# V of the last block's two groups issued from GpSimd's queue instead of SyncE's

## The chip, the cores and the metric

The kernel runs on one core of a Trainium2 chip. A core has a tensor engine (TensorE, PE in the profile; its weight loads are listed as PEld), a vector engine (VectorE, DVE), a scalar engine (ScalarE, ACT), GpSimd (POOL) and SyncE (SP), which does nothing but issue DMA transfers. Each engine works through its own list of instructions in order; engines wait for each other by semaphores. Transfers are moved by 16 DMA engines of the core, whichever engine issued them. The metric is the device time of one execution in microseconds (us), the median of several.

## The reference

Attention within chunks of 64 positions, over 8 batches, 8 heads, 576 positions and a head size of 64, and then a feed-forward part with a squared ReLU on the 4608 x 512 result:

```python
q_c, k_c, v_c = (z.reshape(B, H, S // 64, 64, D) for z in (q, k, v))
scores = np.matmul(q_c, k_c.transpose(0, 1, 2, 4, 3)) / np.sqrt(D)
attn = np.exp(scores - scores.max(-1, keepdims=True))
attn = attn / (attn.sum(-1, keepdims=True) + 1e-09)
x = np.matmul(attn, v_c)            # (B, H, S, D) -> (B*S, H*D) = (4608, 512)
h = np.maximum(x @ w_in, 0.0)       # w_in: 512 x 2048
out = (h * h) @ w_out               # w_out: 2048 x 512
```

All inputs and the output are float32 in HBM.

## The kernel before

The 4608 tokens are cut into 18 groups of 256 (`GT`), each of four chunks of 64; two groups make a block, so there are nine blocks, 0 to 8. Groups are numbered from 0 as well: block 8 holds groups 16 and 17, block 7 groups 14 and 15. Most groups are four neighbouring chunks of one batch ("whole"); groups 14 and 15 are gathered from the ninth chunk of each batch, so their loads come in twice as many pieces.

For one group the steps are: load Q, K and V; cast Q and K to bfloat16 (`CQ`, `CK`; both: `C`; lines L449 and L454, on GpSimd for the blocks that matter here); transpose both by one DMA (`TD`, L460, issued by SyncE); scores on TensorE and the exponential on ScalarE (`SC`, L483 and L494); the product with V in two halves (`AV0`, `AV1`, L510), with a division by the sums on VectorE (L442, L443); and the transpose of the result x (`XT`), which for blocks 6 to 8 is a DMA that SyncE issues (L535). The attention of block j+1 is done while the feed-forward part of block j runs.

V of a group lies in SBUF in float32. The even heads go to `v_even[g % 5]` in two pieces of 128 tokens (L308); the odd heads go to tiles of `v_odd`, shifted by a chunk (L312). Group 16 has three odd pieces (64, 128 and 128 tokens), group 17 two (128 and 64). One piece of 128 tokens and four heads is 128 KB, in runs of 256 bytes. Each DMA waits until the readers of the buffer's earlier contents are through.

From block 4 on the feed-forward part works in "quads": a quad is a quarter of the hidden units of a block, and its products are Strassen-like, seven instead of eight (`quad_step`, L657), with sums of x formed by VectorE in `x_sums` (L614). The second of these sums, e2, needs both groups' transposed x of its block, and the product A6 uses it. A quad is spread over one tick of four slots; a block has four quads and so 16 slots. `run(tick)` emits, slot by slot, the quad's products, the second layer's products of the block before (L780), and whatever `plan` has for the slot. At the start of each tick GpSimd squares one ReLU result of the quad before (L676). Stores of results are issued by GpSimd (L809, or L804 for the gathered groups).

The order on each engine's list is thus written out by hand: `at(j, s, f)` puts f at slot s of block j, and a slot above 15 is one of block j+1. The loads of block j+2 are put into the slots of block j. For j = 6 (`n_blk - 3`), which loads block 8, the pieces come from one iterator, `pieces`: Q and K of group 16 (three DMAs), Q and K of group 17 (three), V of group 16 (five), V of group 17 (four); `load(n, more)` issues the next n of them. All are on SyncE, among the transposes that stand in the same slots: XT of group 14 at slot 8 and of group 15 at slot 13, TD of group 16 at 9.5 and of group 17 at 14.5. AV0 of group 16 is planned at slot 2 of block 7, that of group 17 at slot 8.

Of the kernel before, what the change touches and what calls it, by code (L numbers as in the profile page):

```python
# [144 lines left out]
def kernel(  # L145
# [9 lines left out]
    nc = tc.nc  # L155
# [12 lines left out]
    blocks = [[g, g + 1] for g in range(0, n_grp, 2)]  # L168
# [8 lines left out]
    def is_whole(g):  # L177
        return chunks[g][0][0] == chunks[g][3][0]

    FIRST_DMA_T = 4
    X_BY_DMA = (6, 7, 8)
    QUADS = 4
    LEAD = 4
# [61 lines left out]
    def runs(g):  # L247

        for t in range(2):
            (b, s), (b1, s1) = chunks[g][2 * t:2 * t + 2]  # L250
            if b == b1:
                yield t, 0, 2 * CH, b, s
            else:
                yield t, 0, CH, b, s
                yield t, CH, CH, b1, s1
# [6 lines left out]
    def qk_pieces(g):  # L262


        def pairs(which, src, p, m, b, s):
            return lambda: nc.sync.dma_start(  # L266
                out=loaded(g, which)[p:p + m // 2, :].rearrange("p (h e) -> p h e", h=H),
                in_=src[b, :, s:s + m, :].rearrange("h (s i) d -> s h (i d)", i=2))
# [3 lines left out]
        else:  # L272
            for c in range(4):
                yield pairs(0, q, c * CH // 2, CH, *chunks[g][c])
        if g < FIRST_DMA_T:
            yield pairs(1, k, 0, GT, *chunks[g][0])
# [9 lines left out]
    for g in range(n_grp):  # L286
        if is_whole(g):
# [3 lines left out]
            b, s = chunks[g][0]  # L291
# [12 lines left out]
    def v_pieces(g):  # L304

        even, odd = [], []
        for t, p, m, b, s in runs(g):
            even.append(lambda t=t, p=p, m=m, b=b, s=s: nc.sync.dma_start(  # L308
                out=v_even[g % NV][p:p + m, t, :, 0:D],
                in_=v[b, 0::2, s:s + m, :].rearrange("h s d -> s h d")))  # L310
        for n, p, m, b, s in odd_loads[g]:
            odd.append(lambda n=n, p=p, m=m, b=b, s=s: nc.sync.dma_start(  # L312
                out=v_odd[n % NO][p:p + m, :, 0:D],
                in_=v[b, 1::2, s:s + m, :].rearrange("h s d -> s h d")))
        if g < 2:
            yield from [even[0], *odd[:-1], even[1], odd[-1]]
        else:
            yield from even + odd
# [34 lines left out]
    def x_tile(j):  # L353
        if j not in xTs:
            xTs[j] = att_pool.tile([128, BT // 128, n_dt, 128], BF16, name="xT", bufs=2)
        return xTs[j]
# [107 lines left out]
    def scores(g):  # L464
        qkT = state.pop(("qkT", g))
        by_plane = g >= FIRST_DMA_T

# [62 lines left out]
    def transpose_x(g):  # L530
        x = state.pop(("x", g))
        n = 2 * half_of(g)
        dst = x_tile(g // 2)[:, n:n + 2].rearrange("p t h q -> p (t h) q")
        if g // 2 in X_BY_DMA:
            nc.sync.dma_start_transpose(out=dst, in_=x.rearrange("p t h a d -> p (t h a d)"))  # L535
# [15 lines left out]
    for j in range(n_blk):  # L551
        if j < QUADS:
            at = {(th, fh, h): 4 * th + 2 * fh + h
                  for th in range(2) for fh in range(2) for h in range(2)}
        else:
# [6 lines left out]
            at = {(*key, 0): s for key, s in zip(keys, old)}  # L562
# [83 lines left out]
    def tock():  # L646
        state["clock"] += 1
        for x in [x for x in later if x[0] <= state["clock"]]:
            later.remove(x)
            x[1]()  # L650
# [276 lines left out]
    def pieces(grps):  # L927
        for g in grps:
            yield from qk_pieces(g)
        for g in grps:  # L930
            yield from v_pieces(g)
# [72 lines left out]
    for j in range(QUADS):  # L1004
# [3 lines left out]
        def at(slot, f, *x):  # L1008
            plan.setdefault(slot, []).append((f, x))
# [28 lines left out]
        else:  # L1038
# [4 lines left out]
            if j == 2:  # L1043
                loads, go_slots = itertools.chain(*map(v_pieces, nxt), pieces(far)), [
                    *range(16), *range(27, 36)]
                slots = {SC: (6, 10), AV: (12, 22), XT: (15, 28), CQ: (20, 22), CK: (21, 24), TD: (24, 26)}
                for f in (CQ, CK, TD):
                    for i, g in enumerate(far):
                        at(slots[f][i], f, g)
                phases.append(out_j)  # L1050
            else:
                loads, go_slots = pieces(far), range(11)
                at(11, C, far[0])
                at(13, CQ, far[1])
                at(13, TD, far[0])
                slots = {SC: (2, 2), AV: (6, 10), XT: (13, 15)}
# [40 lines left out]
    for j in range(QUADS, n_blk):  # L1097
        if j == QUADS:
            n = 14 - LEAD
            slots = [1 + 19 * i // n for i in range(n)]  # L1100
            assert len(slots) == n
        else:
            slots = [s for s in range(4, 20) if s % 16 not in NO_OUT]
            start = 3
        if j == QUADS:
            g = blocks[QUADS + 1][1]
            between = {0: [(CK, (g, nc.scalar.copy)), (TD, (g,))]}
            for n in (0, 1, 2, 3):
                between.setdefault(n, []).append((load, (1, loads)))
            for n in (2, 2, 2, 3):  # L1110
                between.setdefault(n, []).append((x_sums, (QUADS, len([1 for z in between.values() for y in z if y[0] is x_sums]))))
            for f, x in between.get(0, []):
                f(*x)
            for i in range(LEAD):
                next(out_j)
                tock()
                for f, x in between.get(i + 1, []):
                    f(*x)
        else:
            outs[j - 1] = ffn_out(j - 1)  # L1120
            at(j, start, lambda j=j: next(outs[j - 1])())
        for s in slots:
            plan.setdefault(("out", 16 * (j - QUADS) + s), []).append(outs[j - 1])

        if j + 1 < n_blk:
            S0, V0, V1, X0 = ((1.5, 3.5), (4.5, 7.5), (6, 10), (8.5, 12)) if j == QUADS else (
                (1.5, 7), (3.5, 8), (5, 9.5), (5.5, 10)) if j == QUADS + 1 else (
                (0.5, 7), (2, 8), (3.5, 9.5), (3.5, 10)) if is_whole(blocks[j + 1][0]) else (
                (3.5, 9.5), (5, 11), (7, 12), (8, 13))
            for i, g in enumerate(blocks[j + 1]):  # L1130
                at(j, S0[i], SC, g)
                at(j, V0[i], AV0, g)
                at(j, V1[i], AV1, g)
                at(j, X0[i], XT, g)
            if j + 2 == n_blk:
                at(j, 22, check_sums)
                at(j, 25.5, count_bad)
            for i, s in enumerate((13.5, 16 if j == n_blk - 3 else 15, 17.5, 18)):
                at(j, s, x_sums, j + 1, i)
        if j == QUADS:  # L1140
            for s in range(4):
                at(j, 4 * s + 2, w_sums_in_place, s)
            assert next(loads, None) is None
        if j + 2 < n_blk:
            more = pieces(blocks[j + 2])
            if j == n_blk - 3:

                for s, n in ((0, 1), (1, 1), (2, 1), (8.5, 3), (13, 5), (15, 2), (15.5, 2)):
                    at(j, s, load, n, more)
            else:  # L1150
                for s in range(0, 16):
                    at(j, s, load, 1 if is_whole(blocks[j + 2][0]) else 2, more)
            for i in range(2):
                at(j, (9, 10 if j == QUADS else 13)[i], C, blocks[j + 2][i])
                at(j, ((9.5, 14.5) if j == n_blk - 3 else (12, 13.5))[i], TD, blocks[j + 2][i])
# [66 lines left out]
```

## Time and profile before

| | us |
|---|---|
| median of 3 runs | 277.8 |
| lowest and highest | 277.05, 279.23 |
| the profiled execution, its own time | 276.91 |
| its span in the trace | 275.1 |
| granted TensorE clock in it | 1.00 |

In the profile, a line such as L460 is the line of the kernel's text; SPq marks an issue by SyncE, whose time is that of the issue and not of the transfer. A DMA issued by GpSimd counts as busy time of POOL. Rows of the timeline give start and duration in us, engine, line, operation, what is written and read, and how many rows were merged; in square brackets stand the engine's idle time before it and what ended it. Rows of stretches give the busy time of PE, PEld, DVE, ACT and POOL with the number of instructions, then the granted clock, the share of time in which the 16 DMA engines were busy (packets that overlap count twice, so it can exceed 1), and the GB/s moved. The chain of waits follows the program back from its end, at each step to what released it.

Where the bytes go, by queue (packets, MB, share of 16 engines' time):

```profile
q1 hardware_dynamic: 133248, 46.54, 74.0%
q0 software_dynamic: 2624, 8.39, 9.6%
```

The first is SyncE's queue, the second GpSimd's, which carries stores alone.

### The profile page before, as it was taken

How to read it: one execution, taken by the hardware profiler on the slowest of the kernel's cores; microseconds unless marked ns; L12 is line 12 of the kernel's file. 1: busy time of each engine (PE TensorE's matmuls, PEld its weight loads, DVE VectorE, ACT ScalarE, POOL GpSimd, SP SyncE). 2: the span in 40 equal slices, each digit the busy share in tenths (PEclk: the TensorE clock that was granted, in tenths of full speed). 3: DMA queues.
4: the chain of work that ended last, by engine and by line, in shares of the span. 5: the costliest groups of instructions: out<-in, count | busy, mean ns of one | idle time of the engine just before them, and what ended most of it. 6: DMA issues, size and time to landing. Idle time of an engine off the chain costs nothing.

```text
span 275.1 us, 7923 instructions
## 1 busy us (share of the span) xinstructions
PE 264.9 (96%) x3261; PEld 203.4 (74%) x3261; DVE 199.2 (72%) x365; ACT 168.3 (61%) x300; POOL 89.6 (33%) x122
## 2 busy tenths in 40 slices
PE   2999999999999999999999999999999999999995
PEld 2764445888774588447878888888888888888884
DVE  1457514999538592499989998799779877994752
ACT  1657614894458883877678765565746665756430
POOL 2048834240360012040245224551643212331600
PEclk9999999999999999999999999999999999999999
DMA  7999999999999999999999999697999530220223
GB/s 216 262 352 389 361 332 270 339 213 172 262 210 218 238 234 218 275 223 178 228 236 197 218 238 194 103 220 196 244 187 224 123 76 2 99 55 7 71 83 114
DMA packets 136056, 55.60 MB, mean 202 GB/s; under 512 B 104273, under 2 KB 131921, under 8 KB 136017
## 3 DMA queue, kind: packets, MB, share of 16 engines
q1 hardware_dynamic: 133248, 46.54, 74.0%
q0 software_dynamic: 2624, 8.39, 9.6%
q8 instruction: 26, 0.43, 0.6%
q10 hardware_dynamic: 144, 0.13, 0.1%
q14 instruction: 14, 0.11, 0.1%
HBM read 36.70 MB, written 9.44 MB: 168 GB/s over the span
## 4 chain that ended last, share of the span: by engine, by line
PE 87%; DMA 4%; SPq 3%; DVE 3%; ACT 1%; issue 1%; ACTq 0%; DVEq 0%
PE ps_ffn L657 22%; PE ps_out L780 22%; PE ps_ffn L579 17%; PE ps_ffn L780 14%; PE ps_ffn L901 5%; PE ps_att L510 3%; PE ps_att L540 2%; DMA vo_sb<-in_v_dram 2%; PE ps_att L483 2%; DMA xT<-x 2%; DVE gT L598 2%; SPq L266 1%; SPq L308 1%; SPq L312 1%; DVE x L443 1%; ACT e L494 1%
## 5 line engine op out<-in xcount | busy, mean ns | idle before, releaser
L579 PE MATMUL ps_ffn<-xT,w_in_bf 128*128 128x512 bf16 (+1 forms) x328 | 57.8, 333 | 0.0
L780 PEld LDWEIGHTS <-w_st 128*128 128x128 bf16 x512 | 48.9, 98 | 6.6 <-DVE w_st L614 0.5
L665 DVE CUSTOM_DVE_ANT_0 relu<-ps_ffn,w_st 128x512 f32<-128x512 f32 x60 | 39.3, 684 | 13.0 <-PE ps_ffn L657 11.6
L579 PEld LDWEIGHTS <-w_in_bf 128*128 128x128 bf16 x328 | 31.2, 98 | 21.6 <-POOL w_in_bf L334 0.2
L598 DVE TENSOR_TENSOR gT<-relu 128x256 bf16<-128x256 bf16 (+2 forms) x68 | 34.1, 537 | 17.8 <-ACT relu L590 17.3
L590 ACT ACTIVATE relu<-ps_ffn 128x256 bf16<-128x256 f32 (+2 forms) x82 | 39.4, 501 | 9.4 <-PE ps_ffn L579 8.6
L657 PE MATMUL ps_ffn<-qk_st,w_in_bf 128*128 128x256 bf16 x240 | 35.3, 273 | 0.1
L657 PEld LDWEIGHTS <-w_in_bf 128*128 128x128 bf16 x320 | 30.7, 98 | 4.1 <-issue 0.3
L809 POOL DMA_DIRECT2D out_dram<-o_sb x24 | 17.6, 733 | 43.6 <-DVE o_sb L614 23.3
L780 PEld LDWEIGHTS <-gT 128*128 128x128 bf16 x296 | 28.6, 98 | 3.3
L780 PE MATMUL ps_out<-w_out_bf,w_st 128*128 128x256 bf16 x240 | 30.8, 273 | 0.0
L699 ACT ACTIVATE w_st<-ps_ffn 128x512 f32<-128x512 f32 x20 | 11.9, 597 | 29.6 <-PE ps_ffn L657 29.6
L443 DVE TENSOR_TENSOR x<-ps_att,recs 128x512 bf16<-128x512 f32 x36 | 24.9, 692 | 1.2
L657 PEld LDWEIGHTS <-qk_st 128*128 128x128 bf16 x240 | 22.6, 98 | 3.2 <-DVE qk_st L614 0.3
L657 PE MATMUL ps_ffn<-xT,qk_st 128*128 128x256 bf16 x160 | 23.9, 273 | 0.0
L676 POOL TENSOR_TENSOR qk_st<-relu 128x512 bf16<-128x512 f32 x10 | 10.3, 1034 | 41.6 <-DVE relu L665 38.1
L494 ACT ACTIVATE e<-ps_att 128x1024 bf16<-128x1024 f32 x18 | 18.3, 1025 | 8.5 <-PE ps_att L483 8.5
L676 POOL TENSOR_TENSOR gT<-relu 128x512 bf16<-128x512 f32 x10 | 10.3, 1033 | 35.4 <-DVE relu L665 30.5
L449 POOL CAST qkb<-qk_st 128x1024 bf16<-128x1024 f32 x12 | 13.0, 1082 | 14.9 <-DMA qk_st<-in_q_dram 14.9
L674 ACT ACTIVATE gT<-relu 128x512 bf16<-128x512 f32 x28 | 17.7, 631 | 0.0
L780 PE MATMUL ps_ffn<-w_out_bf,w_st 128*128 128x256 bf16 x144 | 17.7, 273 | 0.0
L614 DVE TENSOR_TENSOR w_st<-gT,w_st 128x1024 bf16<-128x1024 bf16 x26 | 16.8, 682 | 0.0
(92 smaller groups left out, 428.7 us busy)
## 6 DMA issues: line engine op xcount, KB each, us to landing
qk_st<-in_q_dram SPq DMA_DIRECT2D x16, 512.0 KB, 5.6
out_dram<-o_sb POOLq DMA_DIRECT2D x28, 256.0 KB, 3.9
qk_st<-in_k_dram SPq DMA_DIRECT2D x24, 256.0 KB, 5.6
ve_sb<-in_v_dram SPq DMA_DIRECT2D x32, 128.0 KB, 3.9
w_st<-in_moe_w_in_dram SPq DMA_DIRECT2D x8, 512.0 KB, 5.9
w_st<-in_moe_w_out_dram SPq DMA_DIRECT2D x8, 512.0 KB, 5.5
vo_sb<-in_v_dram SPq DMA_DIRECT2D x24, 128.0 KB, 3.6
qk_st<-in_k_dram SPq DMA_DIRECT2D x4, 512.0 KB, 5.8
```

What stands on the lines that cost most here:

```text
L443: nc.vector.tensor_tensor(out=x, in0=o[:, :, :, 0:D], in1=rec.to_broadcast([128, 2, n, D]), op=ALU.mult)
L494: nc.scalar.activation(out=e_out, in_=s_in, func=AF.Exp, scale=scale)
L579: nc.tensor.matmul(out=h[:, 0:n], lhsT=w_in_bf[:, dt, ft * 128:(ft + 1) * 128], rhs=xT[:, c // 128:(c + n) // 128, dt, :], start=(dt == 0) ...
L590: nc.scalar.activation(out=rl[:, 0:n], in_=h[:, 0:n], func=AF.Relu)
L598: nc.vector.tensor_tensor(out=dst, in0=src, in1=src, op=ALU.mult)
L614: nc.vector.tensor_tensor(out=out, in0=in0, in1=in1, op=op)
L657: nc.tensor.matmul(out=bank[:, f * GT:(f + 1) * GT], lhsT=a[:, dt, ft * 128:(ft + 1) * 128], rhs=b[:, :, dt, :], start=(first and f == 0 a ...
L665: nc.vector._custom_dve(TENSOR_ADD_SAT, out=out, in0=in0, in1=in1, s0=BIG, s1=0.0)
L674: engine.activation(out=dst, in_=r, func=AF.Square)
L676: engine.tensor_tensor(out=dst, in0=r, in1=r, op=ALU.mult)
L780: nc.tensor.matmul(out=out_ps, lhsT=lhsT, rhs=b[:, i, :], start=(first and i == 0 and (last or t == 0)), stop=(i == HF - 1), skip_group_ch ...
L809: dma.dma_start(out=out[t0:t0 + GT, col:col + HD].rearrange("(t p) d -> p t d", p=128), in_=o_sb.rearrange("p (t d) -> p t d", d=HD))
```

## The change

V of groups 16 and 17 is issued by GpSimd. The five pieces of group 16 stand at slot 4.5 of block 6 instead of slot 13, where they were behind XT of group 15; the four of group 17 stand at slot 18 of block 6, which is slot 2 of block 7, instead of slots 15 and 15.5. Q and K of both groups keep their slots and their order on SyncE.

```diff
@@ -180,6 +180,7 @@
     FIRST_DMA_T = 4
+    V_BY_GPSIMD = (16, 17)
     X_BY_DMA = (6, 7, 8)
@@ -304,12 +305,13 @@
     def v_pieces(g):
 
         even, odd = [], []
+        dma = nc.gpsimd if g in V_BY_GPSIMD else nc.sync
         for t, p, m, b, s in runs(g):
-            even.append(lambda t=t, p=p, m=m, b=b, s=s: nc.sync.dma_start(
+            even.append(lambda t=t, p=p, m=m, b=b, s=s: dma.dma_start(
                 out=v_even[g % NV][p:p + m, t, :, 0:D],
                 in_=v[b, 0::2, s:s + m, :].rearrange("h s d -> s h d")))
         for n, p, m, b, s in odd_loads[g]:
-            odd.append(lambda n=n, p=p, m=m, b=b, s=s: nc.sync.dma_start(
+            odd.append(lambda n=n, p=p, m=m, b=b, s=s: dma.dma_start(
                 out=v_odd[n % NO][p:p + m, :, 0:D],
                 in_=v[b, 1::2, s:s + m, :].rearrange("h s d -> s h d")))
@@ -1144,9 +1146,11 @@
         if j + 2 < n_blk:
             more = pieces(blocks[j + 2])
             if j == n_blk - 3:
-
-                for s, n in ((0, 1), (1, 1), (2, 1), (8.5, 3), (13, 5), (15, 2), (15.5, 2)):
-                    at(j, s, load, n, more)
+                more = itertools.chain(*map(qk_pieces, blocks[j + 2]))
+                last_v = itertools.chain(*map(v_pieces, blocks[j + 2]))
+                for s, n, which in ((0, 1, more), (1, 1, more), (2, 1, more), (4.5, 5, last_v),
+                                    (8.5, 3, more), (18, 4, last_v)):
+                    at(j, s, load, n, which)
```

## The prediction, made before the changed kernel ran

> **What bounds the kernel now.** I read the page first, then the waits of TensorE in the middle of the program, then the chain of waits around the one wait that was left, and last the two issuing queues around it.
>
> ```profile
> span 275.1 us, 7923 instructions
> PE 264.9 (96%) x3261; PEld 203.4 (74%) x3261; DVE 199.2 (72%) x365; ACT 168.3 (61%) x300; POOL 89.6 (33%) x122
> ```
>
> TensorE is busy for 264.9 of 275.1 us, so 10.2 us of idle time is all that any change of order could give back, and it matters where those 10.2 us lie. The waits of PE alone, asked for 130 to 258 us (the quad stage, in which blocks 4 to 8 run and all that the diff moves is issued), answer with one row:
>
> ```profile
> PE ps_ffn L657 <- DVE qk_st L614: 0.2, 1, 0.2
> ```
>
> In 128 us TensorE waited once, for 0.2 us. The other idle time lies in the first loads and the last block, which the diff does not touch. The chain of waits around that one wait shows what it hangs on (start, duration, what):
>
> ```profile
> 201.12 4.81 DMA xT<-x
> ...
> 206.02 0.56 DVE qk_st L614
> ...
> 206.62 1.05 PE ps_ffn L657 x8
> ```
>
> The transposing DMA of x of block 7's second group (I call it XT15) is issued at 201.12, lands 4.81 us later at 205.93, VectorE forms the sum e2 from it until 206.58, and the A6 product of block 7's first quad starts at 206.62. There is no slack: a microsecond more on XT15's landing is a microsecond of idle TensorE, while a microsecond less gives 0.2 us. SyncE's queue shows what stands ahead of XT15 and what behind:
>
> ```profile
> 188.18 0.61 SPq L266 DMA_DIRECT2D qk_st<-in_q_dram  x1
> 188.85 2.31 SPq L279 DMA_DIRECT2D qk_st<-in_k_dram  x2
> 191.32 2.76 SPq L535 DMA_TRANSPOSE xT<-x  x1
> 194.13 0.58 SPq L266 DMA_DIRECT2D qk_st<-in_q_dram  x1
> 194.75 1.49 SPq L279 DMA_DIRECT2D qk_st<-in_k_dram  x2
> 196.50 4.52 SPq L460 DMA_TRANSPOSE qkT<-qkb  x1
> 201.12 1.74 SPq L535 DMA_TRANSPOSE xT<-x  x1
> 202.91 1.37 SPq L308 DMA_DIRECT2D ve_sb<-in_v_dram  x2
> 204.33 1.83 SPq L312 DMA_DIRECT2D vo_sb<-in_v_dram  x3
> 206.26 3.53 SPq L460 DMA_TRANSPOSE qkT<-qkb  x1
> 209.84 2.09 SPq L308 DMA_DIRECT2D ve_sb<-in_v_dram  x2
> 211.97 1.86 SPq L312 DMA_DIRECT2D vo_sb<-in_v_dram  x2
> 213.93 1.37 SPq L535 DMA_TRANSPOSE xT<-x  x1
> ```
>
> In order: Q and K of group 16, XT14, Q and K of group 17, the transpose of group 16's Q and K (TD16), XT15, then V of group 16, TD17, V of group 17, XT16. From 188.18 to 206.16 the list never stands still for more than 0.3 us. The nine V loads that leave it all stand behind XT15.
>
> **The change, part by part.** First, what SyncE loses: five issues between 202.91 and 206.16 and four between 209.84 and 213.83. XT15 is ahead of them, so its issue gains nothing. TD17 can rise by at most 206.26 − 202.91 = 3.35 us, and nothing in the waits shows TensorE standing for it; XT16 waits for its x in any case. Gain on the path: nothing.
>
> Second, what GpSimd gains. Its own list around the two places, with its idle time in brackets:
>
> ```profile
> 184.04 1.03 POOL L676 TENSOR_TENSOR qk_st<-relu 128x512 bf16<-128x512 f32 x1 [3.21 <-DVE relu L665]
> 185.02 0.75 POOL L809 DMA_DIRECT2D out_dram<-o_sb  x1
> 190.95 1.03 POOL L676 TENSOR_TENSOR qk_st<-relu 128x512 bf16<-128x512 f32 x1 [5.18 <-DVE relu L665]
> 192.74 1.54 POOL L449 CAST qkb<-qk_st 128x1024 bf16<-128x1024 f32 x1 [0.77 <-DMA qk_st<-in_q_dram]
> 195.43 1.04 POOL L454 CAST qkb<-qk_st 128x1024 bf16<-128x1024 f32 x1 [1.15 <-DMA qk_st<-in_k_dram]
> ...
> 205.25 1.04 POOL L676 TENSOR_TENSOR gT<-relu 128x512 bf16<-128x512 f32 x1 [2.92 <-DVE relu L665]
> 206.23 1.47 POOL L809 DMA_DIRECT2D out_dram<-o_sb  x2
> 212.02 1.03 POOL L676 TENSOR_TENSOR gT<-relu 128x512 bf16<-128x512 f32 x1 [4.32 <-DVE relu L665]
> ```
>
> Squares fall at the start of each tick of four slots. The casts of group 16 are planned at block 6's slot 9 and stand behind the square at 190.95, which is therefore that of slot 8; the one at 184.04 is that of slot 4, and the one at 205.25, two ticks after 190.95, that of slot 16. The five loads of group 16 therefore come after 184.04 + 1.03, with the store at 185.02 at their side, in the 5.18 us that GpSimd then stood idle; the four of group 17 come beside the two stores at 206.23, in the 4.32 us before 212.02.
>
> No load by GpSimd is in the trace. Its nearest rows are its stores; L804 writes 128 rows of 1 KB and L809 256 of them (duration in ns, lowest, median, highest):
>
> ```profile
> L809 POOL DMA_DIRECT2D out_dram<-o_sb x24: 707/738/751, 69.9 to 239.0; - x24
> L804 POOL DMA_DIRECT2D out_dram<-o_sb x8: 603/612/656, 245.0 to 260.9; - x8
> ```
>
> 128 more rows cost 738 − 612 = 126 ns. A V load of 128 tokens is 4 heads x 128 = 512 rows of 256 bytes: 738 + 2 x 126 = 990 ns is my estimate; one of 64 tokens has 256 rows, 738 ns. Bounds for the large one: 612 ns if rows did not count, 2 x 738 = 1476 ns if cost went by rows alone. I take 990, the line through both rows. Group 16 then costs 4 x 0.99 + 0.74 = 4.70 us, group 17 3 x 0.99 + 0.74 = 3.71 us. From 185.77 (185.02 + 0.75) the first five end at 190.47, before the square of 190.95; from 207.70 (206.23 + 1.47) the other four end at 211.41, before 212.02. (At the lower bound, 612 ns, both stretches end sooner still.) At the upper bound the first five take 4 x 1.476 + 0.74 = 6.64 us and end at 192.41; the square and the cast of Q behind them (1.03 + 1.54) end at 194.98, still before the cast of K16 that waited for its data until 195.43. What is queued behind the new issues (square, cast of Q16, cast of K16, on which TD16 waits) is thus covered on both bounds, by idle time and by the landing of K16. The loads wait for buffers whose readers belong to blocks 5 and 6, whose attention is over by then: no wait is added.
>
> Third, whether V comes in time at its new places. Landing after issue of SyncE's V loads of L308 from 176 to 212 us; then the first products with V of group 16 and of group 17:
>
> ```profile
> DMA to landing us min/median/max: 2.4/3.8/5.0
> ```
>
> ```profile
> 208.48 0.22 PE L510 MATMUL ps_att<-ve_sb,e 64*64 64x65 bf16 x2
> ...
> 218.42 0.22 PE L510 MATMUL ps_att<-ve_sb,e 64*64 64x65 bf16 x2
> ```
>
> Group 16's last load, issued by 190.47, is in by 190.47 + 5.0 = 195.5 at the slowest of these, 13 us ahead of 208.48. Group 17's last is in by 211.41 + 5.0 = 216.4, 2.0 us ahead of 218.42. Cost: nothing.
>
> Fourth, what the moved bytes meet. This is the term that I charge. Group 16's V is 4.5 x 128 KB = 0.59 MB. It moved behind XT15; now it moves ahead of it, beside Q and K of group 16. The DMA engines' share and rate (the last two figures of each row; shares over 1 are overlapping packets):
>
> ```profile
> 187.00:191.00 4.00, 4.00 (x52) 3.39 (x50) 3.90 (x8) 2.87 (x6) 0.05 (x1) 1.00 0.55 141
> 191.00:201.00 10.00, 10.00 (x147) 8.39 (x146) 8.38 (x14) 5.34 (x10) 6.35 (x7) 1.00 1.16 259
> 203.00:204.00 1.00, 1.00 (x11) 0.90 (x10) 0.21 (x1) 0.29 (x2) 0.00 (x0) 1.00 1.00 223
> ```
>
> While group 16's V was moving (203 to 204) the engines were full at 223 GB/s, so it needs 0.59 MB / 223 GB/s = 2.65 us of all engines. From 187 to 191 they were 0.55 full: 0.45 x 4.00 = 1.80 us is free. From 191 to 201 they were full. So 2.65 − 1.80 = 0.85 us of V's traffic spills into the full stretch, in which K16, XT14, Q17, K17, TD16 and XT15 land one after the other, and pushes XT15's landing from 205.93 to about 206.8. TensorE then waits 0.2 + 0.85 us at A6. The bounds: nothing, if all of it finds room (186 to 187, or the holes while the transposes run); 2.65 us if none does. I take 0.85, since the free stretch is where GpSimd issues. The Trainium skill, DMA: Bandwidth & Descriptors, section "Issuing engines are not separate DMA queues", says that DMAs of all issuing engines run on the same 16 DMA engines and interleave, so that a second issuer saves issue time alone. By that rule the sum is the one just made; a reading by queues, in which GpSimd's own queue costs SyncE's nothing, would make it 0. The trace has no load of this size by GpSimd beside a full SyncE queue, so no run shows it yet.
>
> After A6 the rows show no later wait of TensorE to absorb a delay, so it goes to the end. The sum: −0 (SyncE) + 0 (GpSimd) + 0 (V in time) + 0.85 (contention) = +0.85 us. The profiled execution took 276.91 us, 1.8 over its span and 0.9 below the median of the runs, 277.8; its forecast is 277.75, and the median's 277.8 + 0.85 = 278.65, say 278.6.
>
> **The rivals.** A: V finds room everywhere and nothing moves, 277.8, or 277.6 with the one wait of 0.2 gone. For it: the spill is the small difference of two estimates, and the free stretch need not begin at 187 sharp. Against it: zero slack at A6.
>
> B: the whole of V goes ahead of Q16 and K16, because GpSimd's queue is served as well as SyncE's, and SyncE's issues also lengthen (K16's two took 2.31 us and TD16 4.52 where the lists were full): +1.5 to +2.7 us, 279.3 to 280.5.
>
> C, the slow side: a V issue holds GpSimd for longer than any store. With c for a 128 KB load, GpSimd is free at 185.77 + 4.5c, the square and two casts add 1.03 + 1.54 + 1.04, and TD16, whose issue took 2.42 us at its shortest,
>
> ```profile
> L460 SPq DMA_TRANSPOSE qkT<-qkb x4: 2418/3712/4518, 176.8 to 206.3; - x4
> ```
>
> lets XT15 go at 191.80 + 4.5c. That is past 201.12 from c = 2.07 us on, and costs 1% (2.8 us) from c = 2.69 us: 280.6 and up. For it: VectorE is busy for 3.90 of the 4.00 us from 187 to 191, and GpSimd shares something with it (its cast at 192.74 took 1.54 where another took 1.04). Against it: 24 stores among such work stay within 707 to 751 ns. The Trainium skill, SBUF — State Buffer, section "SBUF: two separate sides", warns of just this: while VectorE runs an operation that holds the shared ports, GpSimd cannot write descriptors, and a DMA of 620 ns took about 3100. By that figure c would be 3.1 and the cost 4.5 x 3.1 − 9.32 = 4.6 us, an estimate from that page; the stores' rows above do not agree with it.
>
> D: something not in these rows (a wait for V17, whose cover is only 2.0 us, or a reordering of GpSimd's stores), either way.
>
> **How the numbers follow.** Forecast, +0.3 to +1.5 us: 0.47. A: 0.28. B: 0.10. C: 0.08. D: 0.07. What a measurement of this kernel can tell from no change is about 1%, 2.8 us. Slower by more: C and half of D, 0.12. Faster by more: only through D, since TensorE has no such time to give back in this stage, 0.02. Within: 0.86. The range runs from 277.0 (A with the runs' own scatter, 277.05 to 279.23) to 280.6 (the top of B, where C decides); outside remain C, most of D and a few hundredths of A, under 0.2.
>
> **What would show it.** In the profile after: five GpSimd rows of L308 and L312 of about 0.74 to 1.0 us between 185 and 191, and four near 207 to 212; the square at about 190.9 still there; XT15 landing at about 206.8 and a wait of TensorE at A6 of about 1 us; TD17 at about 203. If that wait is still 0.2 us, the contention term is wrong and A holds. If the issues take over 2 us each and the casts of group 16 are late, C holds. If TensorE waits at the first products with V of group 17, it is D.

## The result: 0.4% slower, and the profile after

| | before | changed |
|---|---|---|
| median of 22 runs each, us | 277.9 | 279.15 |
| lowest and highest, us | 276.74, 281.12 | 277.45, 281.94 |
| ratio, with its 95% interval | | 1.0043 (1.0023 to 1.0064) |
| timed again, 12 runs against 35 | 277.8 | 279.17 |
| ratio, with its 95% interval | | 1.0043 (1.0016 to 1.0071) |

The ratio is 1.2 us on 277.9, between 0.6 and 1.8 us. All ratios, here and below, leave out executions that took over 1.5% longer than the fastest of the same kernel. The rows that follow are of a second profile of the changed kernel, taken with the second timing; in the first the TensorE clock dropped for some microseconds, which the last section tells. This execution took 280.97 us with a span of 279.2 us, 1.8 us over the median; part of that arose in the first loads, which the change does not touch, so places are compared by their distance from GpSimd's square at slot 4 of block 6 (184.04 before, 186.68 here). Line numbers are one or two higher than before: L462 is the transpose of Q and K, L537 that of x, L310 and L314 are the V loads, L811 the stores.

The page's busy times:

```profile
span 279.2 us, 7923 instructions
PE 265.5 (95%) x3261; PEld 203.1 (73%) x3261; DVE 199.1 (71%) x365; ACT 168.8 (60%) x300; POOL 95.6 (34%) x131
```

The waits of PE from 130 to 263 us (who waited for whom: total, times, longest), where there was one row of 0.2 us:

```profile
PE ps_ffn L659 <- DVE qk_st L616: 1.5, 1, 1.5
PE ps_ffn L659 <- DVE relu L667: 0.3, 1, 0.3
```

And the chain of waits around the first of them:

```profile
206.76 3.28 DMA xT<-x
...
210.13 0.44 DVE qk_st L616
...
210.62 1.05 PE ps_ffn L659 x8
```

The wait for a ReLU result (0.3 us) lies at 151 us, ahead of all that the change moves. The chain is the same as before, with XT15 at its head and A6 at its end, but TensorE now stands for 1.5 us at A6. XT15 lands at 210.04, 23.4 us after the square; before, it was 205.93 − 184.04 = 21.9 us. SyncE's list:

```profile
188.43 2.59 SPq L314 DMA_DIRECT2D vo_sb<-in_v_dram  x4
191.07 0.60 SPq L267 DMA_DIRECT2D qk_st<-in_q_dram  x1
191.73 3.26 SPq L280 DMA_DIRECT2D qk_st<-in_k_dram  x2
195.16 3.50 SPq L537 DMA_TRANSPOSE xT<-x  x1
198.70 0.57 SPq L267 DMA_DIRECT2D qk_st<-in_q_dram  x1
199.31 1.66 SPq L280 DMA_DIRECT2D qk_st<-in_k_dram  x2
201.10 5.56 SPq L462 DMA_TRANSPOSE qkT<-qkb  x1
206.76 1.26 SPq L537 DMA_TRANSPOSE xT<-x  x1
208.11 2.04 SPq L462 DMA_TRANSPOSE qkT<-qkb  x1
```

The issues of K16 take 3.26 us where they took 2.31, XT14 3.50 for 2.76, TD16 5.56 for 4.52: SyncE's list slows down ahead of XT15 though it has lost nine entries, all of them behind XT15. GpSimd's list:

```profile
186.68 1.03 POOL L678 TENSOR_TENSOR qk_st<-relu 128x512 bf16<-128x512 f32 x1 [3.20 <-DVE relu L667]
187.66 1.54 POOL L310 DMA_DIRECT2D ve_sb<-in_v_dram  x2
189.19 2.12 POOL L314 DMA_DIRECT2D vo_sb<-in_v_dram  x3
191.30 0.71 POOL L811 DMA_DIRECT2D out_dram<-o_sb  x1
193.59 1.03 POOL L678 TENSOR_TENSOR qk_st<-relu 128x512 bf16<-128x512 f32 x1 [1.57 <-DVE relu L667]
197.07 1.07 POOL L451 CAST qkb<-qk_st 128x1024 bf16<-128x1024 f32 x1 [2.45 <-DMA qk_st<-in_q_dram]
200.04 1.04 POOL L456 CAST qkb<-qk_st 128x1024 bf16<-128x1024 f32 x1 [1.90 <-DMA qk_st<-in_k_dram]
```

The five loads take 3.66 us and stand ahead of the store, which goes out 191.30 − 186.68 = 4.6 us after the square instead of 185.02 − 184.04 = 1.0. GpSimd does not hold up the casts of group 16: before each it waits for the data (2.45 and 1.90 us, where it was 0.77 and 1.15). The cast of K16 starts 13.4 us after the square, 2.0 later than before (195.43 − 184.04 = 11.4). The DMA engines' stretches (the last two figures: share and GB/s):

```profile
186.00:187.00 1.00, 1.00 (x27) 0.87 (x14) 0.77 (x2) 1.00 (x2) 0.32 (x1) 1.00 2.97 190
187.00:188.00 1.00, 1.00 (x18) 0.72 (x19) 1.00 (x2) 0.43 (x1) 1.00 (x2) 1.00 0.21 5
188.00:191.00 3.00, 3.00 (x42) 2.66 (x43) 2.97 (x7) 2.18 (x5) 3.00 (x5) 1.00 0.98 223
191.00:201.00 10.00, 10.00 (x160) 8.22 (x158) 7.73 (x14) 6.17 (x12) 4.08 (x5) 1.00 1.16 228
189.64:193.64 4.00, 4.00 (x52) 3.39 (x50) 3.90 (x8) 2.87 (x6) 2.43 (x5) 1.00 1.23 226
```

From 188 on the engines are full. The last row is the stretch that lies as far behind the square as 187 to 191 did before, from which the prediction took 1.80 us of free time: its share is 1.23 where it was 0.55, its rate 226 GB/s where it was 141. Ahead of it, from 187 to 188, next to nothing moved. By queue, the same bytes of V also went in other pieces (packets, MB, share of 16 engines' time):

```profile
q1 hardware_dynamic: 129008, 45.49, 72.6%
q0 software_dynamic: 3024, 9.44, 10.7%
```

SyncE's queue lost 133248 − 129008 = 4240 packets and 1.05 MB, GpSimd's gained 3024 − 2624 = 400 packets for the same 1.05 MB.

### The profile page after: what moved, and what is told of

Its sections match the earlier page's. It is cut to its first block, busy times and chain, and to the rows that moved or that the text cites. A ratio compares the mean times of both kernels' runs of the same rounds, so it can differ in the third digit from the quotient of the medians.

```text
span 280.2 us, 7920 instructions
## 1 busy us (share of the span) xinstructions
PE 266.7 (95%) x3258; PEld 204.1 (73%) x3261; DVE 197.5 (70%) x365; ACT 168.6 (60%) x300; POOL 96.2 (34%) x131
## 3 DMA queue, kind: packets, MB, share of 16 engines
q1 hardware_dynamic: 129008, 45.49, 71.5%
q0 software_dynamic: 3024, 9.44, 11.1%
## 4 chain that ended last, share of the span: by engine, by line
PE 69%; DMA 17%; SPq 5%; DVE 3%; POOL 2%; ACT 1%; issue 1%; DVEq 0%; ACTq 0%
PE ps_ffn L659 22%; PE ps_out L782 22%; PE ps_ffn L782 10%; PE ps_ffn L581 8%; DMA w_st<-in_moe_w_out_dram 5%; DMA qkT<-qkb 5%; DMA w_st<-in_moe_w_in_dram 4%; PE ps_att L512 2%; DMA qk_st<-in_k_dram 2%; DVE gT L600 2%; PE ps_att L485 1%; PE ps_att L542 1%; SPq L267 1%; DMA xT<-x 1%; PE ps_ffn L903 1%; SPq L310 1%
## 5 line engine op out<-in xcount | busy, mean ns | idle before, releaser
L667 DVE CUSTOM_DVE_ANT_0 relu<-ps_ffn,w_st 128x512 f32<-128x512 f32 x60 | 39.3, 685 | 13.3 <-PE ps_ffn L659 11.9
L600 DVE TENSOR_TENSOR gT<-relu 128x256 bf16<-128x256 bf16 (+2 forms) x68 | 33.9, 530 | 19.2 <-ACT relu L592 18.8
L581 PEld LDWEIGHTS <-w_in_bf 128*128 128x128 bf16 x328 | 31.0, 98 | 21.8 <-POOL w_in_bf L336 0.7
L782 PE MATMUL ps_out<-w_out_bf,w_st 128*128 128x256 bf16 x240 | 31.9, 279 | 0.0
L811 POOL DMA_DIRECT2D out_dram<-o_sb x24 | 17.5, 732 | 41.7 <-DVE o_sb L616 22.0
L659 PEld LDWEIGHTS <-qk_st 128*128 128x128 bf16 x240 | 22.6, 98 | 4.5 <-DVE qk_st L616 1.6
L659 PE MATMUL ps_ffn<-xT,qk_st 128*128 128x256 bf16 x160 | 23.9, 273 | 0.0
L451 POOL CAST qkb<-qk_st 128x1024 bf16<-128x1024 f32 x12 | 13.0, 1086 | 20.2 <-DMA qk_st<-in_q_dram 20.2
L456 POOL CAST qkb<-qk_st 128x1024 bf16<-128x1024 f32 x11 | 12.9, 1177 | 13.4 <-DMA qk_st<-in_k_dram 13.4
```

The lines of the kernel that those rows point to most:

```text
L451: copy(out=qkb[:, 0].rearrange("p (i h d) -> p i h d", i=2, h=H), in_=loaded(g, 0).rearrange("p (h i d) -> p i h d", h=H, i=2))
L581: nc.tensor.matmul(out=h[:, 0:n], lhsT=w_in_bf[:, dt, ft * 128:(ft + 1) * 128], rhs=xT[:, c // 128:(c + n) // 128, dt, :], start=(dt == 0) ...
L600: nc.vector.tensor_tensor(out=dst, in0=src, in1=src, op=ALU.mult)
L659: nc.tensor.matmul(out=bank[:, f * GT:(f + 1) * GT], lhsT=a[:, dt, ft * 128:(ft + 1) * 128], rhs=b[:, :, dt, :], start=(first and f == 0 a ...
L667: nc.vector._custom_dve(TENSOR_ADD_SAT, out=out, in0=in0, in1=in1, s0=BIG, s1=0.0)
L782: nc.tensor.matmul(out=out_ps, lhsT=lhsT, rhs=b[:, i, :], start=(first and i == 0 and (last or t == 0)), stop=(i == HF - 1), skip_group_ch ...
```

## The experiments

Where one number places the loss, it is the stretch from the square at slot 4 of one block to that of the next, read from GpSimd's timeline. Blocks 4 to 5 (22.1 to 22.6 us) and 7 to 8 (26.0 or 26.1, but for one kernel) are nearly the same in all fourteen profiles. The table has the other two, with the start of the cast of K16, the issue and landing of TD16 and the landing of XT15, in us after the square at slot 4 of block 6.

| kernel | block 5 to 6 | block 6 to 7 | cast K16 | TD16 issue, landing | XT15 landing | ratio (95% interval) |
|---|---|---|---|---|---|---|
| before | 26.1 | 28.0 | 11.4 | 12.5, 21.0 | 21.9 | |
| before, timed as an experiment | 26.1 | 28.0 | 10.9 | 12.3, 20.0 | 20.7 | 0.9991 (0.9973 to 1.0009) |
| changed, first profile | 26.1 | 31.4 | 13.9 | 15.7, 22.5 | 23.9 | 1.0043 (1.0023 to 1.0064) |
| changed, second profile | 26.1 | 29.3 | 13.4 | 14.4, 22.0 | 23.4 | 1.0043 (1.0016 to 1.0071) |
| first group only | 26.1 | 31.3 | 13.3 | 14.7, 22.3 | 23.7 | 1.0032 (1.0009 to 1.0055) |
| second group only | 26.1 | 28.0 | 11.1 | 12.3, 20.9 | 21.8 | 1.0028 (1.0000 to 1.0057) |
| the same again | 26.1 | 28.0 | 11.6 | 12.8, 21.1 | 22.0 | 1.0012 (0.9993 to 1.0031) |
| five tiny loads | 26.1 | 29.8 | 12.2 | 13.4, 21.6 | 22.5 | 1.0024 (0.9988 to 1.0060) |
| V16 at slot 7 of block 5 | 26.1 | 31.7 | 14.8 | 15.9, 24.8 | 25.7 | 1.0210 (1.0163 to 1.0258) |
| V16 at slot 10 of block 5 | 27.2 | 28.2 | 11.5 | 12.6, 21.4 | 22.2 | 1.0030 (1.0004 to 1.0055) |
| V16 early by SyncE | 26.1 | 33.5 | 11.1 | 17.5, 24.3 | 25.9 | 1.0150 (1.0122 to 1.0178) |
| V16 behind the casts | 26.1 | 33.2 | 10.6 | 12.2, 25.0 | 25.7 | 1.0064 (1.0023 to 1.0105) |
| Q, K of group 17 behind XT15 | 26.1 | 33.9 | 13.6 | 14.6, 22.3 | 23.2 | 1.0110 (1.0065 to 1.0156) |
| all nine V loads early | 26.1 | 32.3 | 15.3 | 17.4, 23.5 | 24.8 | 1.0192 (1.0155 to 1.0229) |

**The changed kernel again.** No edit.

> The changed kernel as it is, for a profile at full clock and for a second timing. Theory T (group 16's V moves through the DMA engines ahead of the transpose XT15, and TensorE waits for it at A6): ratio to before 1.003 to 1.007, TensorE idle 0.5 to 1.5 us at block 7's first A6 product. If the longer time of the first profile was clock alone, the ratio is 1.00 here and the wait 0.2 us.

Ratio 1.0043, a wait of 1.5 us at A6 with the clock at 1.00: the loss is that wait, not the clock.

**Which group's V.** First group 16 alone, then group 17 alone, the latter twice.

```diff
-    V_BY_GPSIMD = (16, 17)
+    V_BY_GPSIMD = (16,)
-                                    (8.5, 3, more), (18, 4, last_v)):
+                                    (8.5, 3, more), (15, 2, last_v), (15.5, 2, last_v)):
```

> Group 16's V early by GpSimd, group 17's by SyncE at its old slots. Theory T: all of the loss is here, ratio 1.003 to 1.007, the wait at A6 as in the changed kernel. Rival S (the loss comes with group 17's V, whose issues by GpSimd stand among the stores and whose absence lets TD17 rise): 1.000, wait at A6 0.2 us.

```diff
-    V_BY_GPSIMD = (16, 17)
+    V_BY_GPSIMD = (17,)
-                for s, n, which in ((0, 1, more), (1, 1, more), (2, 1, more), (4.5, 5, last_v),
-                                    (8.5, 3, more), (18, 4, last_v)):
+                for s, n, which in ((0, 1, more), (1, 1, more), (2, 1, more), (8.5, 3, more),
+                                    (13, 5, last_v), (18, 4, last_v)):
```

> Group 17's V by GpSimd at slot 18, group 16's by SyncE at its old slot 13. Theory T: nothing new stands ahead of XT15, ratio 0.998 to 1.002, one wait of 0.2 us at most at A6. Rival S: 1.003 to 1.007.

> Group 17's V alone by GpSimd, timed once more, beside the kernel before against itself. Its first ratio was 1.0028 (1.0000 to 1.0057) while its profile had no wait beyond the 0.2 us at A6. Theories T and K: not to be told from the kernel before's own ratio. Rival S: above it by 0.002 or more.

Group 16 alone brings the wait at A6 back (1.4 us, and 0.4 us at the scores of group 16), with 1.0032. Group 17 alone leaves the stretch from block 6 to 7 at 28.0 us, as before, in both profiles, and the only wait of TensorE behind the moved loads is the 0.2 us at A6 that was there before. Its two ratios, 1.0028 and 1.0012, have intervals that reach 1.0000 and 0.9993, while the kernel before against itself gave 0.9991. So the wait is group 16's; whether group 17's move costs a tenth of a per cent stays open.

**The issues without the bytes.** The kernel before, with

```diff
+                at(j, 4.5, lambda: [nc.gpsimd.dma_start(out=x, in_=v[0, 0, 0:128, i:i + 1])
+                                    for i, x in enumerate(vt_scratch)])
```

> The kernel before with five more loads by GpSimd at slot 4.5, each of 128 runs of 4 bytes into a tile that nothing reads; V stays with SyncE. The issues are there, 2.5 KB in place of 576 KB move. Theory T: ratio 0.998 to 1.002. Rival G (GpSimd is held by its issues, and the casts of group 16 and TD16 come late): 1.002 to 1.007, with the cast of K16 starting later after its square than before.

The timing is no verdict (0.9988 to 1.0060). The profile is not what theory T expected: GpSimd's timeline and the waits of PE from 130 to 263 us show

```profile
185.35 2.72 POOL L1151 DMA_DIRECT2D scratch<-in_v_dram  x5
188.06 0.72 POOL L810 DMA_DIRECT2D out_dram<-o_sb  x1
```

```profile
PE ps_att L511 <- DMA vo_sb<-in_v_dram: 1.1, 1, 1.1
PE ps_ffn L658 <- DVE qk_st L615: 0.7, 1, 0.7
```

The five issues also push the store of 256 KB back, to 188.06, 3.7 us after the square. XT15 lands at 22.5, later than in the kernels without early loads (20.7 to 22.0), and the cast of K16 starts at 12.2, where those have 10.9 to 11.6. The sign that was set for rival G is thus there, but not for its reason: GpSimd itself is not held, it idles 1.40 us for K16's data before that cast. The wait of 1.1 us is for V of group 16, which SyncE loads here, behind XT15. So part of the delay of Q and K comes without V's bytes. Whether the moved store, the 640 reads of 4 bytes or the stop of the DMA engines that this profile shares with the changed kernel (last section) makes it was not tried apart.

**V16 in a gap of the DMA engines.** The changed kernel with group 16's V in block 5; slot 7 was meant for the gap of 173 to 178 us, and was too early (159 us); with slot 10 they went out just ahead of it.

```diff
-                for s, n, which in ((0, 1, more), (1, 1, more), (2, 1, more), (4.5, 5, last_v),
+                for s, n, which in ((0, 1, more), (1, 1, more), (2, 1, more), (-9, 5, last_v),
```

> The changed kernel, but group 16's V by GpSimd at slot 7 of block 5, before the stretch of 173 to 178 us in which the DMA engines of the kernel before were 0.35 to 0.60 busy, instead of slot 4.5 of block 6. As many issues by GpSimd, as many bytes ahead of XT15. Theory T in its narrow form (what counts is whether the bytes find free time of the engines): about 2.65 us are free there, the wait at A6 goes back to 0.2 us or near it, ratio 0.998 to 1.002. Rival (any V by GpSimd ahead of XT15 costs the same, by issue or by queue): 1.003 to 1.007.

The second time with -6 for -9:

> As the run before that was meant for the gap of 173 to 178 us, but at slot 10 of block 5: slot 7 stood a tick too early, at 159 us, where the DMA engines were full. GpSimd is idle there from 168.3 to 171.8 in the kernel before, so the five loads go out in that time and their 0.59 MB land from 172 on, with about 2.65 us of the engines free up to 178. Theory T: nothing then lies beside Q16 and K16, TensorE waits 0.2 us at A6, ratio 0.997 to 1.003. If V by GpSimd ahead of XT15 costs by its number of issues or its queue: 1.003 to 1.007. If the bytes meet V and the transposes of block 7 instead, a wait for TD14 or TD15 shows up, ratio over 1.003.

At slot 7 the loads went out at 159.4 us, far ahead of the gap, and the delay ran down the whole list: TD14 landed 186.4 us, TensorE stood 3.7 us for it at the scores of group 14, and the ratio is 1.0210. At slot 10 they went out from 168.5 to 172.1. Q16 and K16 are on time again (cast of K16 at 11.5, XT15 at 22.2). The waits of PE, from 150 to 200 us and from 200 to 230 us:

```profile
PE ps_ffn L659 <- DVE qk_st L616: 0.7, 1, 0.7
```

```profile
PE ps_ffn L659 <- DVE qk_st L616: 0.4, 1, 0.4
```

The wait at block 7's A6 is nearly gone, as theory T has it, but the A6 of block 6 now waits 0.7 us: its own transpose, XT13, landed at 179.6 instead of 174.8, among V's bytes. The ratio, 1.0030, is not better than the changed kernel's by more than the intervals. The loss went where V16 went; whether by its bytes or by its issues, this run does not part.

**The same slot by SyncE.** Only `V_BY_GPSIMD = (17,)`; group 16's five loads stay at slot 4.5.

> Group 16's V at slot 4.5 of block 6 as in the change, but issued by SyncE. Theory T: the same bytes at the same place plus five issues of about 0.6 us each ahead of XT14 in SyncE's list, so XT15 is later than in the changed kernel: wait at A6 2 to 4 us, ratio 1.008 to 1.016. Rival Q (GpSimd's queue is what costs, its packets going ahead of SyncE's): 1.000 to 1.003.

Ratio 1.0150, waits of 2.3 us at the scores of group 16 and then 1.7 us at A6, where 2 to 4 were expected at A6 alone. Rival Q falls: the same bytes in the same slot cost more through SyncE, not less. The place is not quite the same, for SyncE's list lags behind its slots: V16 goes out 7.8 us after the square, behind K16, where GpSimd issues it 1.0 us after. So K16 is cast in time (11.1), and TD16 is still issued at 17.5, behind V16, XT14 and group 17's Q and K. Here the list is late and the transfers are not: TD16 takes 6.8 us from issue to landing and XT15 3.3, less than before (8.5 and 4.8).

**V16 behind the casts.** Slot 9.5 of block 6, by GpSimd.

```diff
-                for s, n, which in ((0, 1, more), (1, 1, more), (2, 1, more), (4.5, 5, last_v),
-                                    (8.5, 3, more), (18, 4, last_v)):
+                for s, n, which in ((0, 1, more), (1, 1, more), (2, 1, more), (8.5, 3, more),
+                                    (9.5, 5, last_v), (18, 4, last_v)):
```

> Group 16's V by GpSimd at slot 9.5 of block 6, behind the casts of Q16 and K16, still ahead of XT15. Theory T as predicted (all bytes ahead of XT15 in the full stretch count): 2.65 us of traffic with no free time, wait at A6 1.5 to 2.7 us, ratio 1.005 to 1.010. Theory K (what counts is that Q16 and K16 land late, since the cast of K16 lets TD16 go and XT15 stands behind it): Q16 and K16 have the engines to themselves again, TD16 goes 12.5 us after the square of slot 4 as before, the wait at A6 is under 0.8 us, ratio 0.999 to 1.003.

This is the cleanest of them. SyncE's timeline has TD16 and XT15 issued when they were before (12.2 and 17.1 us after the square, before 12.5 and 17.1), and GpSimd's casts of group 16 are on time:

```profile
196.81 4.83 SPq L462 DMA_TRANSPOSE qkT<-qkb  x1
201.74 1.44 SPq L537 DMA_TRANSPOSE xT<-x  x1
```

But the row of TD16's issue to its landing, first here and then before, is

```profile
DMA to landing us min/median/max: 12.8/12.8/12.8
```

```profile
DMA to landing us min/median/max: 8.5/8.5/8.5
```

and TensorE waits for it and for XT15 behind it:

```profile
PE ps_att L485 <- DMA qkT<-qkb: 2.9, 1, 2.9
PE ps_ffn L659 <- DVE qk_st L616: 0.8, 1, 0.8
```

Neither TD16 nor XT15 is issued late here; the transfers alone are, TD16's by 4.3 us (5.1 against the other profile of the kernel before, 7.7). Further down GpSimd's list does come late, the square of slot 12 by 2.2 us, but TensorE waits for nothing on it. Theory K (only a late K16 counts) had the issue of TD16 and the wait at A6 right (under 0.8; it was 0.78), but not the 2.9 us at the scores, and so it falls; theory T had the size of the loss, but at A6 alone. The ratio, 1.0064, rests on five of the twelve runs; the median of all twelve is 282.72 us, 1.7% over the kernel before. In the profile the clock dropped too (last section).

**Less ahead of XT15.** The changed kernel with Q and K of group 17 moved behind XT15.

```diff
-                                    (8.5, 3, more), (18, 4, last_v)):
+                                    (13, 3, more), (18, 4, last_v)):
```

> The changed kernel with Q and K of group 17 (1 MB) moved from slot 8.5 to slot 13, behind XT15 in SyncE's list. Theory T: XT15 lands about 3 us earlier, the wait at A6 is gone. The casts of group 17 then wait on GpSimd, so TD17 comes late; scores of group 17 need it at slot 7 of block 7, and it may be that a wait turns up there: ratio 0.997 to 1.003, with no wait at A6 in either case. If TensorE still waits 1 us at A6, T is wrong.

TensorE still waits 1.0 us at A6, against the expectation of theory T. With 1 MB less ahead of it XT15 lands at 23.2, hardly sooner than in the changed kernel (23.4). GpSimd's and SyncE's timelines say why:

```profile
199.97 1.04 POOL L456 CAST qkb<-qk_st 128x1024 bf16<-128x1024 f32 x1 [2.71 <-DMA qk_st<-in_k_dram]
```

```profile
201.03 4.84 SPq L462 DMA_TRANSPOSE qkT<-qkb  x1
205.97 1.72 SPq L537 DMA_TRANSPOSE xT<-x  x1
```

K16's data still came late, so TD16 could not go before 201.03, and XT15 stands behind it. (The square of slot 16 waited on GpSimd behind the casts of group 17, so only the two stretches together count: 33.9 + 24.0 = 57.9 us against 54.0.) A transposing DMA can thus be late in two ways, by what it waits for (here) and by what moves beside it (the run before), and V16 at slot 4.5 does the first.

**All nine loads early.** `(4.5, 9, last_v)` in place of the two entries.

> All nine V loads by GpSimd at slot 4.5 of block 6: 1.08 MB instead of 0.59 MB ahead of XT15. Theory T: 0.48 MB at 223 GB/s is 2.1 us more in a stretch that is already full, so the wait at A6 grows by about 2 us over the changed kernel's, ratio 1.010 to 1.016, more if the clock drops in the wait. Rival S or G: no more than the changed kernel, 1.003 to 1.007, since GpSimd is free again before the casts.

1.0192, above what was expected. XT15 lands 1.4 us later than in the changed kernel (24.8 against 23.4), the cast of K16 1.9 us (15.3 against 13.4): more loads, more delay. The wait at A6 did not grow by 2 us, as was expected of theory T: it is 1.4 us, and a wait of 1.5 us at the scores of group 16 stands ahead of it. The clock's drop on top makes the rest of the stretch.

## Why the prediction came out

The forecast was 278.6 against 277.8, +0.8 us; measured was +1.2 us (0.6 to 1.8), to the forecast's side and within its range. The place and the kind of the loss were foreseen. That the size lies so near is in part luck: the term that makes it was too small, and the way it takes was another. Step by step:

- **The place.** Right. The loss is at A6 of block 7, behind XT15, in the stretch that begins with the moved loads, and group 16's V makes it (1.0032 alone, with the same wait).
- **No slack, 0.2 us to be had.** Wrong as a statement on the kernel. The kernel before in its other profile had XT15 in at 205.4 (20.7 us after the square), 1.2 us sooner, with the same 0.2 us of waiting. VectorE's timeline there shows that e2 came from VectorE's own queue, right behind another sum:

```profile
205.83 0.69 DVE L614 TENSOR_TENSOR o_sb<-ps_out,kept 128x512 f32<-128x512 f32 x1
206.44 0.74 DVE L614 TENSOR_TENSOR qk_st<-qk_st,xT 128x512 bf16<-128x512 bf16 x1
```

  In the first profile the landing (205.93) and the end of that sum (205.91) happened to coincide. So in one of the two profiles XT15 had 206.44 − 205.40 = 1.0 us of slack, and the wait that the chain put down to it was not its own.
- **GpSimd's cost.** The row model, 126 ns per 128 rows, failed: loads of 512 runs cost 0.75 to 0.79 us, not 0.99, and those of 256 runs on 64 partitions 0.63. The stores come near the same two values by partitions (738 ns on 128, 612 on 64), so between these the number of partitions tells more than that of runs. It isn't the whole: the tiny loads, 128 partitions with one run of 4 bytes each, took 2.72 / 5 = 0.54 us. Nothing hung on it, since idle time covered either.
- **The store.** Missed. The prediction put it ahead of the loads; it stands behind, and its 256 KB went out 3.6 us later after the square, beside Q16 as well.
- **The contention term.** Right in kind, too small: XT15 came 23.4 − 21.9 = 1.5 us later, where 0.85 was charged, and TensorE waited 1.5 us where 0.2 + 0.85 was forecast. The sum without free time, 2.65 us, is the other end; the measured 1.5 lies between. The free time was about right: 226 − 141 = 85 GB/s more over 4.00 us is 0.34 MB, where 1.80 us at 223 GB/s would have taken 0.40. What the sum did not have is the stop from 187 to 188: 5 GB/s, where at the same distance from the square it was about 200 before (184 to 186). At 223 GB/s those 0.2 MB are 0.9 us, an estimate. It fits the tiny loads, which have that stop and none of V's bytes and cast K16 0.8 us later than before (12.2 against 11.4); but two profiles of the kernel before alone differ there by 0.5 us, so this part is argued, not shown. The 2.65 us, too, was no measure of V alone: from 203 to 204 TD16 and XT15 were in flight as well, and by GpSimd V goes in far fewer packets.
- **The way it takes.** The prediction had the spill travel through a full list of transfers. The profile shows two steps: Q16 and K16 land later (their casts start 1.7 and 2.0 us later), so TD16 is issued 2.0 us later and XT15 3.0 us later. In flight both are quicker than before (7.6 us for 8.5, 3.3 for 4.8), and taking 1 MB out of the list did not help.
- **Rival C** (GpSimd held) is out: it waited for data before each cast. The Trainium skill, SBUF — State Buffer, section "SBUF: two separate sides", warned of a DMA by GpSimd of about 620 ns that takes about 3100 beside a copy by VectorE; these issues took 0.63 to 0.79 us with VectorE 2.97 of 3.00 us busy, so no run here shows it, and whether VectorE's operations here are of that kind, no run tells. **Rival A** is out with the interval. **B** (+1.5 to +2.7) overlaps it at its lower end, and its account is nearer to the profile than the forecast's: V goes ahead of Q16 and K16, and SyncE's issues lengthen (K16's two from 2.31 to 3.26 us).
- **TD17** was to rise to about 203. It was issued 208.11 − 186.68 = 21.4 us after the square, 0.8 us sooner than before: it waits for the cast of K17, whose data came late as well.

The rule that was weighed, the Trainium skill, DMA: Bandwidth & Descriptors, section "Issuing engines are not separate DMA queues", agrees with the runs: in the run behind the casts V16 by GpSimd made SyncE's TD16 take 12.8 us where it took 8.5, though it was issued in time. No version here beats the kernel before.

## What to carry to other kernels

Moving a load to an idle issuing queue frees the old queue only behind the place where it stood; the bytes go to the same DMA engines, so ask which transfer that TensorE waits for is in flight at the new place. A low DMA share may be room, as it was here, and the moved bytes can still delay a transfer that a cast, a transpose and then TensorE wait for in turn; and zero slack in one profile is worth a second profile. A DMA put into a hand-written list also moves what stands behind it there: here a store of 256 KB.

## What the runs showed of the hardware

**Stops of the DMA engines.** In several profiles a row with a share far over 1 is followed by one with almost no traffic: 2.97 and then 5 GB/s in the rows from 186 to 188 above, while TD15 was in flight. The tiny loads have it in the same place, and the kernel before has one elsewhere, beside XT15 (first the tiny loads, then before):

```profile
185.00:186.00 1.00, 1.00 (x25) 0.70 (x23) 1.00 (x3) 0.12 (x1) 1.00 (x3) 1.00 3.00 230
186.00:187.00 1.00, 1.00 (x11) 0.90 (x10) 1.00 (x3) 0.49 (x1) 1.00 (x2) 1.00 0.12 7
```

```profile
201.00:202.00 1.00, 1.00 (x12) 0.90 (x10) 1.00 (x2) 1.00 (x3) 1.00 (x1) 1.00 2.92 232
202.00:203.00 1.00, 1.00 (x12) 0.90 (x10) 1.00 (x2) 0.85 (x2) 0.33 (x1) 1.00 0.06 6
```

In the 4 us after the square of slot 4 in block 6 the stop stands in five of the six profiles with loads by GpSimd at slot 4.5 (both of the changed kernel, group 16 alone, the tiny loads, Q and K of group 17 behind XT15; not with all nine loads), and in none of the other eight. So it goes with loads by GpSimd at this place, not with V's bytes. What causes it, no view tells.

**The clock after two short waits.** In the run with group 16 alone TensorE waited 0.4 us at the scores of group 16 and, right behind them, 1.4 us at A6, and its granted clock (the figure before the share) fell to half for some 3.4 us:

```profile
206.00:208.00 2.00, 0.81 (x36) 0.41 (x33) 0.22 (x1) 0.75 (x1) 2.00 (x3) 1.00 1.06 198
208.00:209.00 1.00, 0.40 (x2) 0.28 (x3) 0.88 (x2) 0.27 (x1) 0.30 (x1) 0.81 1.14 214
209.00:212.00 3.00, 3.00 (x15) 1.98 (x13) 2.01 (x5) 1.71 (x3) 0.00 (x0) 0.50 1.01 244
212.00:213.00 1.00, 1.00 (x23) 0.79 (x23) 0.48 (x2) 0.00 (x0) 0.00 (x0) 0.99 1.24 277
```

That is why its stretch is 31.3 us and that of the changed kernel's second profile, with 1.5 us at A6 alone and no drop, 29.3: half of 3.4 us is 1.7 us on top of the waits. All five profiles with a wait of 0.4 us or more at the scores of group 16 and one at A6 right behind it show the drop: 0.4 and 1.4 us here, 0.5 and 1.5 in the changed kernel's first profile, 2.3 and 1.7 by SyncE, 1.5 and 1.4 with all nine loads, 2.9 and 0.8 behind the casts. Near their waits the others do not: one wait of 1.5 us (the changed kernel's second profile), one of 3.7 us (V16 at slot 7 of block 5), 0.7 and then 1.1 us some 2 us later (the tiny loads), 0.3 and 1.0 us (Q and K of group 17 behind XT15). What exactly sets it off, these runs do not settle.
